# Float16 pairs in the first FFN product, and units of two f tiles: a fused local attention and FFN on one core

## The chip, the cores and the metric

The kernel runs on one core of one Trainium2 chip. The metric is the device time of one execution in microseconds (us); lower is better. Engines are named as the profile names them: PE is TensorE's matmuls and PEld its weight loads, DVE is VectorE, ACT is ScalarE, POOL is GpSimd, SP is the engine whose queue issues the DMAs. A line such as L700 is line 700 of the kernel before.

## The reference

Four batches, eight heads, 768 positions, head size 64. Each query sees the keys at a distance under 16 and, beside them, 24 block keys (the maximum over 32 keys each, with log 32 added to the score) whose values are block means. The 3072 x 512 attention output goes through an FFN of width 2048.

```python
scores_l = scale * np.matmul(q, k.transpose(0, 1, 3, 2))       # masked to |i - j| < 16
scores_s = scale * np.einsum('bhsd,bhnd->bhsn', q, k_sum) + np.log(block)
a = softmax(concatenate([scores_l, scores_s]))                 # spelled out in the original
attn = np.matmul(a, concatenate([v, v_sum]))
x = attn.transpose(0, 2, 1, 3).reshape(3072, 512)
h = x @ w_in                                                   # 512 x 2048
g = h * (1.0 / (1.0 + np.exp(-h)))
out = (g @ w_out).astype(np.float32)                           # 2048 x 512
```

The inputs reach the device as float64, seen there as int64; the kernel takes the weights apart by bits.

## The kernel before

**Precision.** Each factor of an FFN product is kept as a high and a low part, and three products are added up: high by high, high by low, low by high. Both parts are float32r (a float32 that TensorE reads in one pass) in both FFN products. The scores of batches 1 to 3 and their products with v use float16 pairs in the same manner.

**FFN tiling.** Tokens come in 12 chunks of 256 (`CH`); the width 2048 in 16 tiles f of 128 (`NFT`). One step of the FFN, `job_f(i, c, f)`, is one chunk and one f:

- `ffn1` (L700): 4 blocks of the 512 inputs by 3 products, 12 matmuls of 256 columns, each with its own 128x128 weight load, into one half of a PSUM bank `h`;
- ACT takes tanh(h/2) into `t` (L709), DVE makes t = (t + 1)h (L710), which is twice silu, ACT rounds it to `gh` (L711), POOL or DVE takes the rest `gl` = t - gh (L216, a helper of all subtractions);
- `ffn2` (L705): for each of the two 128-token halves 3 matmuls of 512 columns, added up over all f in a PSUM bank;
- after the last f, the bank is copied out times 0.5 (L730 on ACT, L731 on DVE) and stored.

The order is: chunks 0 and 1 over the first 8 tiles f (`QF`), chunks 1 and 0 over the other 8, then one chunk after the other over all 16. So there are 192 steps. `ffn1` of step i waits for `ffn2` of step i - 3 (`APART`); rings of 3 buffers hold `t` (`NT2`) and 4 hold `gh` and `gl` (`NG`). Two chunks of x (`xh`, `xl`) are held at a time.

**Weights.** `job_w(f, kind)` loads the 512 columns of one f tile of one weight matrix (kind 0 is w_in, kind 1 is w_out) by one DMA of 512 KB, rebuilds a float32 from the two words of each float64 in a staging half (ACT L664 and L659, DVE L666), copies it to the high part (ACT L209, DVE L213) and subtracts for the low part (DVE L216). Four staging halves, in two of the three `raw` buffers, are in turn. It is done once, in the first part of the execution; until a weight tile is loaded, its space serves as staging for early attention data.

**Attention** goes by 24 stages of 128 tokens (two for each chunk): scores (L545 in float32 for batch 0, L547 and L548 in float16 pairs after it) of two heads at a time, score + mask and row minimum (DVE L552), exponential and sum (ACT L555), scaling (L566 ACT, L568 POOL, L570 DVE), rest (DVE L594), a DMA transposition, the product with v (L626), and x split into `xh` (ACT L644) and `xl` (DVE L645). Batches 1 to 3 are scaled by powers of two found on the chip (`job_scale`, `v_scale`, whose small matmul is L396), and x is brought back to its own scale at L644 and L645.

**What sets the order.** Nothing is ordered by hand. `Plan` collects all operations with a cost in ns, the engines that may run them, their dependencies and a priority, simulates them several times, and issues them in the order of the best sweep, which also picks the engine where there is a choice. Each engine then runs its own instructions strictly in that order. The priorities hold some twenty offsets (`TUNE`). In the first microseconds idle PE time is filled with matmuls of no use (L286), and spare PSUM bank 6 (`sbank`) takes the scores and the small matmuls; bank 3 joins it when chunk 0 has finished.

Of the kernel before, what the change touches and what calls it, by code (L numbers as in the profile page):

```python
# [34 lines left out]
NFT = DFF // P  # L35
NCT = DM // P
# [9 lines left out]
QF = 8  # L46
AHEAD = 0
NPL = 2
APART = 3
# [153 lines left out]
def local_attn_ffn(ctx: ExitStack, tc: tile.TileContext, qkT, qF, qD, kF, kD, v, vR, w, out):  # L203
# [10 lines left out]

    def less(e, out, in0, in1):
        eng[e].tensor_tensor(out=out, in0=in0, in1=in1, op=ALU.subtract)  # L216
# [10 lines left out]
    wr = [wp.tile([P, DM, 2], U32, name="wt") for _ in range(2 * NFT)] if wide else None  # L227
# [3 lines left out]
    nc.vector.memset(ones, 1.0)  # L231

# [22 lines left out]
    NRAW, NP, NTT, NE, NG, NT2 = 3, 4, 8, 3, 4, 3  # L255
# [21 lines left out]
    xh_t = ring(NSUP, [P, NCT, CH], F32R, "xh")  # L277
    xl_t = ring(NSUP, [P, NCT, CH], F32R, "xl")
    part_t = [const.tile([P, 2, DM], F32, name=f"part{i}") for i in range(NSUP - 2)]
    t_t = ring(NT2, [P, CH], F32, "t")  # L280
    gh_t = ring(NG, [P, CH], F32R, "gh")
    gl_t = ring(NG, [P, CH], F32R, "gl")
# [99 lines left out]
    def v_scale(b, prio):  # L382
# [9 lines left out]
            lambda e: nc.vector.tensor_scalar(out=sc2[:, 3:4], in0=sc2[:, 1:2], scalar1=1.0 / PSC, scalar2=None, op0=ALU.mult))  # L392
# [4 lines left out]
        plan.op({"dve": 67}, lambda e, k=k: nc.vector.tensor_copy(out=vsc_t[b % 2], in_=bank[k][:, :2]), r=[("bank", k)], w=[("vsc", b % 2)], prio=prio)  # L397

# [116 lines left out]
    def tt_of(m):  # L515
        if m < 16 and wide:
            f, kind = tt_late[m // 2 % 4]
            buf, key = wr[2 * f + kind].rearrange("p c i -> p (c i)").bitcast(F32)[:, m % 2 * 4 * P:(m % 2 + 1) * 4 * P], ("w", f, kind, m % 2)
        else:
            return tt_t[m % NTT].rearrange("p (a b) -> p a b", a=6), ("tt", m % NTT)  # L520
        if m < 4 * NPL:
            return buf.rearrange("p (a b) -> p a b", a=4), key
        return buf.bitcast(F16)[:, :6 * P].rearrange("p (a b) -> p a b", a=6), key

    def job_a(m, prio):
# [70 lines left out]
        plan.op({"dve": 672}, low, r=er + sums, w=[("p", pk), ("p", pk, "half")], prio=prio)  # L596
        plan.op({"dma": 672}, lambda e: nc.sync.dma_start_transpose(out=tt, in_=pt.rearrange("p a b -> p (a b)")), r=[("p", pk), ("p", pk, "half")], w=[ttk], prio=prio)

    def job_c(m, prio):
# [28 lines left out]
        plan.op({"pe": 1560}, mm, r=[ttk for _, ttk in parts] + [("v1", s % 2), ("v2", s % 2)], w=[("bank", 7)], prio=prio, cols=2560)  # L628

    def job_x(s, prio):  # L630
# [13 lines left out]
        plan.op({"act": 500}, lambda e: nc.scalar.activation(out=xh, in_=x3, func=AF.Copy, scale=by), r=[("bank", k), vk], w=[("xh", z, half)], prio=prio)  # L644
        plan.op({"dve": 602}, lambda e: nc.vector.scalar_tensor_tensor(out=xl, in0=x3, scalar=by, in1=xh.bitcast(F32), op0=ALU.mult, op1=ALU.subtract),  # L645
                r=[("bank", k), ("xh", z, half), vk], w=[("xl", z, half)], prio=prio, port=())

    def job_w(f, kind, prio):
        prio += nudge("w", f, kind)
        (wf, key), src = half_staging(), w[f][:, kind * DM:(kind + 1) * DM]  # L650
        if wide:
            rt = wr[2 * f + kind]
            low, top = rt[:, :, 0], rt[:, :, 1]
            wu = wf.bitcast(U32)
            plan.op({"dma": 1650}, lambda e: nc.sync.dma_start(out=rt.rearrange("p c i -> p (c i)"), in_=src.bitcast(U32)), w=[("w", f, kind)] + [("w", f, kind) + x for x in ((0,), (1,), (0, "side"), (1, "side"))], prio=prio - TUNE["w_dma"] + nudge("wd", f, kind))
# [6 lines left out]


            plan.op({"act": 575}, lambda e: nc.scalar.activation(out=wf, in_=top.bitcast(F32), func=AF.Prelu, scale=REBIAS, alpha=-SIGN), r=[("w", f, kind)], w=key, prio=prio)  # L664
            plan.op({"act": 575, "dve": 335}, last_bits, r=[("w", f, kind)], w=[("wb", f, kind)], prio=prio)
            plan.op({"dve": 602}, lambda e: nc.vector.scalar_tensor_tensor(out=wu, in0=wu, scalar=3, in1=low, op0=ALU.logical_shift_left, op1=ALU.bitwise_or), r=[("w", f, kind), ("wb", f, kind)], w=key, prio=prio)  # L666
# [7 lines left out]
        plan.op({"act": 527, "dve": 335}, hi, r=key, w=[("w", f, kind), "walloc"], prio=prio)
        prio += nudge("wl", f, kind)
        plan.op({"dve": 602}, lambda e: less(e, wt[f, kind][:, 1, :], wf, wt[f, kind][:, 0, :].bitcast(F32)),
                r=key + [("w", f, kind)], w=[("wl", f, kind)], prio=prio)

    first = list(range(NFT))[:QF]
    rest = list(range(NFT))[QF:]  # L680
# [4 lines left out]
    need_c = {c: order.index((c, 0)) for c in range(NCHUNK)}  # L685
    need_f = {f: min(i for i, cf in enumerate(order) if cf[1] == f) for f in range(NFT)}

    def job_f(i, c, f):
        late = i + TUNE["ffn2"] + nudge("f2", i)
        k, j, n, z = nxt("h", 2) if c < NSUP else nxt("late h", 3), i % NT2, i % NG, slot[c]  # L690
        h, t, gh, gl = bank[k][:, :CH], t_t[j], gh_t[n], gl_t[n]
# [3 lines left out]
        opens, closes = f == 0 or (split and f == QF), f == NFT - 1 or (split and f == QF - 1)  # L695

        def ffn1(e):
            for ct in range(NCT):
                for q, (part, x) in enumerate(((0, xh), (0, xl), (1, xh))):
                    nc.tensor.matmul(out=h, lhsT=wt[f, 0][:, part, ct * P:(ct + 1) * P], rhs=x[:, ct, :], start=(ct == 0 and q == 0), stop=(ct == NCT - 1 and q == 2))  # L700

        def ffn2(u):
            def go(e):
                for q, (g, part) in enumerate(((gh, 0), (gh, 1), (gl, 0))):
                    nc.tensor.matmul(out=bank[ob[u]], lhsT=g[:, u * P:u * P + P], rhs=wt[f, 1][:, part, :], start=(opens and q == 0), stop=(closes and q == 2))  # L705
# [3 lines left out]
        plan.op({"act": 264}, lambda e: nc.scalar.activation(out=t, in_=h, func=AF.Tanh, scale=0.5), r=[("bank", k)], w=[("t", j)], prio=i - TUNE["post"])  # L709
        plan.op({"dve": 335}, lambda e: nc.vector.scalar_tensor_tensor(out=t, in0=t, scalar=1.0, in1=h, op0=ALU.add, op1=ALU.mult), r=[("bank", k)], w=[("t", j)], prio=i - TUNE["post"], port=())  # L710
        plan.op({"act": 307}, lambda e: nc.scalar.copy(out=gh, in_=t), r=[("t", j)], w=[("gh", n)], prio=i - TUNE["post"])  # L711
# [156 lines left out]
```

## Time and profile before

| | |
|---|---|
| time, median of 3 runs | 690.64 us (688.04, 690.64, 694.74) |
| profiled execution | span 694.0 us, from the first to the last instruction; no time of its own beside the span is given for it |
| busy time | PE 667.1, PEld 574.5, DVE 478.4, ACT 432.2, POOL 203.0 us |
| granted TensorE clock, mean | 0.982 |
| read from and written to HBM | 70.34 MB and 6.29 MB |

The span of the profiled execution lies 3.4 us above the median and within the three runs. Busy time of PE is the union of matmuls that overlap in a pipeline, so that PE may be marked busy where it isn't at its peak: the distance from the start of one matmul to the start of the next says more. In the views, a group's row ends with its busy time and the mean length of one instruction, and after a second bar the idle time of the engine before it and who ended that.

### The profile page before, as it was taken

The page shows a single profiled execution, that of the slowest core. Times are in us where ns is not written, and L with a number is a line of the kernel's source. Part 1 is how long each engine was busy: PE and PEld are TensorE (multiplying, and loading weights), DVE is VectorE, ACT ScalarE, POOL GpSimd, SP SyncE. Part 2 cuts the span into 40 slices and gives each one's busy share as a digit, 9 for nine tenths or more (in the row PEclk, how much of TensorE's full clock was granted, in tenths as well). Part 3 has the DMA queues.
Part 4 walks back from the last instruction along what each step waited for, and adds up shares of the span by engine and source line. Part 5 has one row for each costly group of instructions (what it writes and reads, how often), then busy time and mean ns, then how long its engine had stood idle before and what let it go on. Part 6 is the DMA issues. An engine that isn't in the chain of part 4 may idle for free. (4 is left out here: it accounts for less than half of the span.)

```text
span 694.0 us, 14248 instructions
## 1 busy us (share of the span) xinstructions
PE 667.1 (96%) x4941; PEld 574.5 (83%) x4941; DVE 478.4 (69%) x1493; ACT 432.2 (62%) x1141; POOL 203.0 (29%) x267
## 2 busy tenths in 40 slices
PE   8998899999989999999999999999999999999997
PEld 3667779888878798878888888888889888999996
DVE  4688978688799657978894556978895883423332
ACT  4779999686667746756675536767864753422322
POOL 2142156335634042425351111415341230000000
PEclk9679999999999999999999999999999999999999
DMA  7869893967667843774675423665573250100000
GB/s 259 292 152 253 306 323 103 219 180 183 159 147 116 244 119 100 199 136 118 142 192 151 125 85 115 178 141 155 139 171 106 52 114 30 43 1 1 32 1 30
DMA packets 101354, 97.41 MB, mean 140 GB/s; under 512 B 76950, under 2 KB 80022, under 8 KB 101282
## 3 DMA queue, kind: packets, MB, share of 16 engines
q1 hardware_dynamic: 101282, 96.51, 52.5%
q8 instruction: 38, 0.62, 0.4%
q14 instruction: 34, 0.28, 0.1%
HBM read 70.34 MB, written 6.29 MB: 110 GB/s over the span
## 5 line engine op out<-in xcount | busy, mean ns | idle before, releaser
L700 PE MATMUL bank<-xh,wt 128*128 128x256 f32 x1536 | 309.5, 285 | 4.1 <-DVE t L710 2.8
L700 PEld LDWEIGHTS bank<-xh,wt 128*128 128x128 f32 x1536 | 251.6, 191 | 13.9 <-DVE t L710 4.3
L705 PE MATMUL bank<-wt,gh 128*128 128x512 f32 x768 | 247.6, 404 | 2.1 <-ACT gh L711 2.1
L700 PE MATMUL bank<-xl,wt 128*128 128x256 f32 x768 | 217.1, 283 | 0.0
L216 POOL TENSOR_TENSOR gl<-t,gh 128x256 fp32r<-128x256 f32 x115 | 98.1, 855 | 269.0 <-ACT gh L711 218.2
L705 PE MATMUL bank<-wt,gl 128*128 128x512 f32 x384 | 151.1, 393 | 1.6 <-DVE gl L216 1.2
L700 PEld LDWEIGHTS bank<-xl,wt 128*128 128x128 f32 x768 | 146.6, 191 | 6.2
L705 PEld LDWEIGHTS bank<-wt,gh 128*128 128x128 f32 x768 | 131.0, 190 | 20.7 <-ACT gh L711 3.0
L710 DVE SCALAR_TENSOR_TENSOR t<-t,bank 128x256 f32<-128x256 f32 x192 | 79.6, 416 | 85.8 <-ACT t L709 84.7
L709 ACT ACTIVATE t<-bank 128x256 f32<-128x256 f32 x192 | 72.3, 377 | 83.3 <-PE bank L700 81.6
L711 ACT CAST gh<-t 128x256 fp32r<-128x256 f32 x192 | 76.9, 402 | 67.2 <-DVE t L710 66.4
L594 DVE SCALAR_TENSOR_TENSOR p<-e,sum,p 128x128 f16<-128x128 f32 x352 | 109.7, 373 | 4.1 <-ACT p L566 2.6
L555 ACT ACTIVATE e<-e,mx 128x182 f32<-128x182 f32 x192 | 84.1, 439 | 31.2 <-DVE mx L552 29.3
L705 PEld LDWEIGHTS bank<-wt,gl 128*128 128x128 f32 x384 | 72.4, 189 | 20.7 <-POOL gl L216 2.5
L216 DVE TENSOR_TENSOR gl<-t,gh 128x256 fp32r<-128x256 f32 x77 | 37.5, 488 | 33.9 <-ACT gh L711 16.9
L568 POOL TENSOR_SCALAR p<-e,sum 128x182 f16<-128x182 f32 x77 | 35.5, 468 | 75.9 <-DVE sum L561 44.8
L552 DVE CUSTOM_DVE_ANT_0 e<-bank,masks,qsc 128x182 f32<-128x182 f32 x144 | 53.2, 399 | 6.5 <-PE bank L548 6.1
L216 POOL TENSOR_TENSOR vv<-raw,vv 128x1024 f16<-128x1024 f32 x16 | 35.2, 2202 | 13.0 <-ACT t L709 6.7
L566 ACT ACTIVATE p<-e,sum 128x182 f16<-128x182 f32 x81 | 33.6, 440 | 7.5 <-issue 3.6
L555 ACT ACTIVATION_READ_ACCUMULATOR e<-e,mx 128x1 f32 x192 | 36.2, 189 | 0.0
L451 DVE SCALAR_TENSOR_TENSOR qk<-raw,qsc,qk 64x1264 f16<-64x1264 f32 x18 | 28.6, 1588 | 8.8 <-ACT qk L450 8.4
L547 PE MATMUL bank<-qk 128*128 128x182 f16 x144 | 28.4, 245 | 4.8 <-DVE mx L552 2.5
(123 smaller groups left out, 685.3 us busy)
## 6 DMA issues: line engine op xcount, KB each, us to landing
wt<-in_w_dram SPq DMA_DIRECT2D x32, 512.0 KB
raw<-in_kD_dram SPq DMA_DIRECT2D x18, 632.0 KB
raw<-in_v_dram SPq DMA_DIRECT2D x20, 512.0 KB
raw<-in_qD_dram SPq DMA_DIRECT2D x18, 512.0 KB
out_dram<-raw SPq DMA_DIRECT2D x24, 256.0 KB
raw<-in_kF_dram SPq DMA_DIRECT2D x12, 384.0 KB
raw<-in_qF_dram SPq DMA_DIRECT2D x9, 512.0 KB
raw<-in_vR_dram SPq DMA_DIRECT2D x12, 384.0 KB
```

Source lines behind the costliest of these rows:

```text
L216: eng[e].tensor_tensor(out=out, in0=in0, in1=in1, op=ALU.subtract)
L451: plan.op({"dve": 1450}, lambda e: nc.vector.scalar_tensor_tensor(out=kst[64:, :, :NLOC], in0=kr[64:], scalar=qs[64:, 1:2], in1=kst[64:, : ...
L552: plan.op({"dve": 258 if b == 0 else 323}, lambda e, i=i: nc.vector.tensor_tensor_reduce(out=et[:, i, :], in0=sc[:, i, :NKEY], in1=mask, s ...
L555: plan.op({"act": 431}, lambda e, i=i, h=h: nc.scalar.activation(out=et[:, i, :], in_=et[:, i, :], func=AF.Exp, scale=-1.0, bias=mx[:, i:i ...
L566: nc.scalar.activation(out=out, in_=et[:, i, :], func=AF.Copy, scale=by)
L568: nc.gpsimd.tensor_scalar(out=out, in0=et[:, i, :], scalar1=by, scalar2=0.0, op0=ALU.mult, op1=ALU.add)
L594: nc.vector.scalar_tensor_tensor(out=pt[:, i, to:to + z - a], in0=et[:, i, a:z], scalar=su[:, i:i + 1], in1=pt[:, i, a:z], op0=ALU.mult, o ...
L700: nc.tensor.matmul(out=h, lhsT=wt[f, 0][:, part, ct * P:(ct + 1) * P], rhs=x[:, ct, :], start=(ct == 0 and q == 0), stop=(ct == NCT - 1 an ...
L705: nc.tensor.matmul(out=bank[ob[u]], lhsT=g[:, u * P:u * P + P], rhs=wt[f, 1][:, part, :], start=(opens and q == 0), stop=(closes and q == 2))
L709: plan.op({"act": 264}, lambda e: nc.scalar.activation(out=t, in_=h, func=AF.Tanh, scale=0.5), r=[("bank", k)], w=[("t", j)], prio=i - TUN ...
L710: plan.op({"dve": 335}, lambda e: nc.vector.scalar_tensor_tensor(out=t, in0=t, scalar=1.0, in1=h, op0=ALU.add, op1=ALU.mult), r=[("bank", ...
L711: plan.op({"act": 307}, lambda e: nc.scalar.copy(out=gh, in_=t), r=[("t", j)], w=[("gh", n)], prio=i - TUNE["post"])
```

## The change

1. x and w_in become float16 pairs. x is scaled by a power of two for each batch: `xh` and `xl` take `vsc_t` (batch 0, first two stages) or the constant 1/PSC, and stay scaled. w_in is scaled by a power of two for each pair of f tiles, found on the chip: an absolute maximum on DVE, two small matmuls that add it up over the partitions, one bit operation. tanh undoes both scales (`asc_t`, one value per unit and batch); what is left of x's scale goes into the copy of the output. `ffn2` keeps float32r; w_out is scaled by the inverse power.
2. Two neighbouring f tiles form one unit: `ffn1` fills the two halves of one PSUM bank (two groups of 12 matmuls), and tanh, t, gh and gl handle 512 columns at once; `ffn2` adds 6 matmuls for each token half. `QF`, `APART`, `NT2` and `NG` become 4, 2, 2 and 3 units.
3. Weights are loaded and converted by pairs, 1024 columns at a time, with DMAs of 1 MB; two whole staging buffers are in turn.
4. Some costs given to `Plan` and all the offsets in `TUNE` have other values.

The core of the diff:

```diff
+NFP = NFT // 2
-QF = 8
+QF = 4
-APART = 3
+APART = 2
+    def times(e, out, in_, by):       # ACT Copy with scale, POOL or DVE tensor_scalar
+    def rest_of(out, in_, by, less):
+        nc.vector.scalar_tensor_tensor(out=out, in0=in_, scalar=by, in1=less, op0=ALU.mult, op1=ALU.subtract)
-    NRAW, NP, NTT, NE, NG, NT2 = 3, 4, 8, 3, 4, 3
+    NRAW, NP, NTT, NE, NG, NT2 = 3, 4, 8, 3, 3, 2
-    xh_t = ring(NSUP, [P, NCT, CH], F32R, "xh")
+    xh_t = ring(NSUP, [P, NCT, CH], F16, "xh")
-    t_t = ring(NT2, [P, CH], F32, "t")
+    t_t = ring(NT2, [P, 2 * CH], F32, "t")
-    def half_staging():
-        i = nxt("half", 2 * (NRAW - 1))
+    def low_staging():
+        i = nxt("low", NRAW - 1)
+        return raw[i][:, :2 * DM], [("raw", i, 0), ("raw", i, 1)]
...
+        by, need = (vsc_t[b % 2][:, 0:1], [("vsc", b % 2)]) if s < NPL else (1.0 / PSC, [])
+        plan.op({"act": 575}, lambda e: times(e, xh, x3, by), ...)
+        plan.op({"dve": 661}, lambda e: rest_of(xl, x3, by, xh), ...)
...
+            plan.op({"dma": 3300}, lambda e: nc.sync.dma_start(out=rt.rearrange("p c i -> p (c i)"), in_=src.bitcast(U32)), ...)
+        u, r = ur_t[:, fp, 0:1], ur_t[:, fp, 1:2]
+        if kind == 0:
+            plan.op({"dve": 1160}, lambda e: nc.vector.tensor_reduce(out=wm_t[:, fp:fp + 1], in_=wf, axis=AX.X, op=ALU.max, apply_absolute_value=True), ...)
+            k = sbank()
+            def gather(e):
+                nc.tensor.matmul(out=bank[k][:, :2], lhsT=spread, rhs=wm_t[:, fp:fp + 1].to_broadcast([P, 2]), start=True, stop=False)
+                nc.tensor.matmul(out=bank[k][:, :2], lhsT=spread, rhs=least.to_broadcast([P, 2]), start=False, stop=True)
+            plan.op({"pe": 240}, gather, ...)
+            plan.op({"dve": 170}, ... out=ur_t[:, fp, :] ... bitwise_and 0x7F800000, bitwise_xor flip ...)
+            plan.op({"pool": 250, "dve": 130}, lambda e: times(e, asc_t[0][:, fp:fp + 1], u, vsc_t[0][:, 1:2]), ...)
+        by = u if kind else r
         def hi(e):
-            copy(e, wt[f, kind][:, 0, :], wf)
+            times(e, flat(0), wf, by)
-                less(e, wt[f, kind][:, 1, :], wf, wt[f, kind][:, 0, :].bitcast(F32))
+                rest_of(flat(1), wf, by, flat(0))
...
+        def ffn1(d):
+            def go(e):
+                for ct in range(NCT):
+                    for q, (part, x) in enumerate(((0, xh), (0, xl), (1, xh))):
+                        nc.tensor.matmul(out=h[:, d * CH:(d + 1) * CH], lhsT=wt[f, 0][:, part, d, ct * P:(ct + 1) * P], rhs=x[:, ct, :], ...)
...
-        plan.op({"act": 264}, lambda e: nc.scalar.activation(out=t, in_=h, func=AF.Tanh, scale=0.5), ...)
+        plan.op({"act": 590}, lambda e: nc.scalar.activation(out=t, in_=h, func=AF.Tanh, scale=asc_t[c // 3 % 2][:, f:f + 1]), ...)
-        plan.op({"pool": 742, "dve": 340}, lambda e: less(e, gl, t, gh.bitcast(F32)), ...)
+        plan.op({"pool": 1280, "dve": 605}, lambda e: less(e, gl, t, gh.bitcast(F32)), ...)
```

More of the change, by code (lines that the diff above doesn't have):

```diff
@@ L213, in copy @@
             eng[e].tensor_copy(out=out, in_=in_)
+    def times(e, out, in_, by):
+        if e == "act":
+            nc.scalar.activation(out=out, in_=in_, func=AF.Copy, scale=by)
+        elif e == "pool":
+            nc.gpsimd.tensor_scalar(out=out, in0=in_, scalar1=by, scalar2=0.0, op0=ALU.mult, op1=ALU.add)
+        else:
+            nc.vector.tensor_scalar(out=out, in0=in_, scalar1=by, scalar2=None, op0=ALU.mult)
+    def rest_of(out, in_, by, less):
+        nc.vector.scalar_tensor_tensor(out=out, in0=in_, scalar=by, in1=less, op0=ALU.mult, op1=ALU.subtract)
     def less(e, out, in0, in1):
@@ L226, in local_attn_ffn, with raw_w @@
     wt = {}
-    wr = [wp.tile([P, DM, 2], U32, name="wt") for _ in range(2 * NFT)] if wide else None
+    wr = [wp.tile([P, 2, DM, 2], U32, name="wt") for _ in range(2 * NFP)] if wide else None
+    def raw_w(f, kind):
+        return wr[2 * (f // 2) + kind][:, f % 2].rearrange("p c i -> p (c i)")
     ident = const.tile([P, P], F32, name="ident")
@@ L231, in local_attn_ffn @@
     nc.vector.memset(ones, 1.0)
+    spread = const.tile([P, P], F32, name="spread")
+    nc.vector.memset(spread, 2.0 ** -13)
+    least = const.tile([P, 1], F32, name="least")
+    nc.vector.memset(least, 2.0 ** -80)
+    flip = const.tile([P, 2], U32, name="flip")
+    nc.vector.memset(flip[:, 0:1], 0)
+    nc.vector.memset(flip[:, 1:2], 0x7F800000)
+    wm_t = const.tile([P, NFP], F32, name="wm")
+    ur_t = const.tile([P, NFP, 2], F32, name="ur")
+    asc_t = [const.tile([P, NFP], F32, name=f"asc{i}") for i in range(2)]
     blocks = const.tile([P, 11 * 4], F32, name="blocks")
@@ L397, in v_scale @@
         plan.op({"dve": 67}, lambda e, k=k: nc.vector.tensor_copy(out=vsc_t[b % 2], in_=bank[k][:, :2]), r=[("bank", k)], w=[("vsc", b % 2)], prio=prio)
+        if b:
+            plan.op({"pool": 250, "dve": 150}, lambda e: times(e, asc_t[b % 2], ur_t[:, :, 0], vsc_t[b % 2][:, 1:2]),
+                    r=[("vsc", b % 2)] + [("ur", f) for f in range(NFP)], w=[("asc", b % 2, f) for f in range(NFP)], prio=prio)
     def job_v(b, prio):
@@ L670, in hi @@
-        def hi(e):
-            wt[f, kind] = wp.tile([P, 2, DM], F32R, name="wt")
-            copy(e, wt[f, kind][:, 0, :], wf)
[L674 to L680, printed above, removed]
+            plan.op({"act": 1000}, lambda e: nc.scalar.activation(out=wf, in_=top.bitcast(F32), func=AF.Prelu, scale=REBIAS, alpha=-SIGN), r=mine, w=key, prio=prio)
@@ L681, in local_attn_ffn @@
+        plan.op({"act": 1040, "dve": 700}, hi, r=key + [("ur", fp)], w=mine + ["walloc"], prio=prio)
+        prio += nudge("wl", fp, kind)
+        plan.op({"dve": 1190}, lambda e: rest_of(flat(1), wf, by, flat(0).bitcast(F32) if kind else flat(0)),
+                r=key + mine + [("ur", fp)], w=[("wl", fp, kind)], prio=prio)
+    first = list(range(NFP))[:QF]
+    rest = list(range(NFP))[QF:]
     runs = [(c, first) for c in range(NSUP)] + [(c, rest) for c in reversed(range(NSUP))]
@@ L684, in local_attn_ffn @@
     slot = [c if c < NSUP else NSUP - 1 - c % NSUP for c in range(NCHUNK)]
-    need_c = {c: order.index((c, 0)) for c in range(NCHUNK)}
-    need_f = {f: min(i for i, cf in enumerate(order) if cf[1] == f) for f in range(NFT)}
+    need_c = {c: 2 * order.index((c, 0)) for c in range(NCHUNK)}
+    need_f = {f: 2 * min(i for i, cf in enumerate(order) if cf[1] == f) for f in range(NFP)}
     def job_f(i, c, f):
-        late = i + TUNE["ffn2"] + nudge("f2", i)
+        at = 2 * i
+        late = at + TUNE["ffn2"] + nudge("f2", i)
         k, j, n, z = nxt("h", 2) if c < NSUP else nxt("late h", 3), i % NT2, i % NG, slot[c]
-        h, t, gh, gl = bank[k][:, :CH], t_t[j], gh_t[n], gl_t[n]
+        h, t, gh, gl = bank[k], t_t[j], gh_t[n], gl_t[n]
         xh, xl = xh_t[z], xl_t[z]
@@ L694, in job_f @@
         split = c < NSUP - 2
[L695 to L700, printed above, removed]
+        opens, closes = f == 0 or (split and f == QF), f == NFP - 1 or (split and f == QF - 1)
@@ L702, in ffn2 @@
+        have = [("w", 2 * f + d, kind) for d in range(2) for kind in range(2)]
+        def ffn1(d):
+            def go(e):
+                for ct in range(NCT):
+                    for q, (part, x) in enumerate(((0, xh), (0, xl), (1, xh))):
+                        nc.tensor.matmul(out=h[:, d * CH:(d + 1) * CH], lhsT=wt[f, 0][:, part, d, ct * P:(ct + 1) * P], rhs=x[:, ct, :], start=(ct == 0 and q == 0), stop=(ct == NCT - 1 and q == 2))
+            return go
         def ffn2(u):
             def go(e):
-                for q, (g, part) in enumerate(((gh, 0), (gh, 1), (gl, 0))):
-                    nc.tensor.matmul(out=bank[ob[u]], lhsT=g[:, u * P:u * P + P], rhs=wt[f, 1][:, part, :], start=(opens and q == 0), stop=(closes and q == 2))
@@ L711, in job_f @@
-        plan.op({"act": 307}, lambda e: nc.scalar.copy(out=gh, in_=t), r=[("t", j)], w=[("gh", n)], prio=i - TUNE["post"])
-        plan.op({"pool": 742, "dve": 340}, lambda e: less(e, gl, t, gh.bitcast(F32)), r=[("t", j), ("gh", n)], w=[("gl", n)], prio=i - TUNE["post"])
+                for d in range(2):
+                    for q, (g, part) in enumerate(((gh, 0), (gh, 1), (gl, 0))):
+                        nc.tensor.matmul(out=bank[ob[u]], lhsT=g[:, d * CH + u * P:d * CH + u * P + P], rhs=wt[f, 1][:, part, d, :], start=(opens and d == 0 and q == 0), stop=(closes and d == 1 and q == 2))
@@ new lines, in ffn2 @@
+            return go
+        for d in range(2):
+            plan.op({"pe": 1310}, ffn1(d), r=[(x, z, half) for x in ("xh", "xl") for half in range(2)] + have[2 * d:2 * d + 1] + [("wl", f, 0)] + ([("turn", i - APART)] if i >= APART else []), w=[("bank", k)], prio=at + nudge("f1", i), cols=3072)
+        plan.op({"act": 590}, lambda e: nc.scalar.activation(out=t, in_=h, func=AF.Tanh, scale=asc_t[c // 3 % 2][:, f:f + 1]), r=[("bank", k), ("asc", c // 3 % 2, f)], w=[("t", j)], prio=at - TUNE["post"])
@@ L713, in job_f @@
+        plan.op({"dve": 605}, lambda e: nc.vector.scalar_tensor_tensor(out=t, in0=t, scalar=1.0, in1=h, op0=ALU.add, op1=ALU.mult), r=[("bank", k)], w=[("t", j)], prio=at - TUNE["post"], port=())
+        plan.op({"act": 515}, lambda e: nc.scalar.copy(out=gh, in_=t), r=[("t", j)], w=[("gh", n)], prio=at - TUNE["post"])
+        plan.op({"pool": 1280, "dve": 605}, lambda e: less(e, gl, t, gh.bitcast(F32)), r=[("t", j), ("gh", n)], w=[("gl", n)], prio=at - TUNE["post"])
         for u in range(2):
-            plan.op({"pe": 690}, ffn2(u), r=[("gh", n), ("gl", n), ("w", f, 1), ("wl", f, 1)], w=[("bank", ob[u])] + ([("turn", i)] if u else []), prio=late, cols=1536)
@@ L715, in job_f @@
-        if closes and f == NFT - 1:
+            plan.op({"pe": 1380}, ffn2(u), r=[("gh", n), ("gl", n), have[1], have[3], ("wl", f, 1)], w=[("bank", ob[u])] + ([("turn", i)] if u else []), prio=late, cols=3072)
+        if closes and f == NFP - 1:
             stg, key = staging()
@@ L778, in local_attn_ffn @@
         job_out(s, False)
-    for f in range(NFT):
+    for f in range(NFP):
         for kind in range(2):
@@ L788, in local_attn_ffn @@
         job_f(i, c, f)
-        if c == 0 and f == NFT - 1:
+        if c == 0 and f == NFP - 1:
             spare[0] = 1
-        if d and f == NFT - 1:
+        if d and f == NFP - 1:
             job_out(2 * d, True)
@@ L795, in local_attn_ffn @@
     plan.issue()
-TUNE = dict(km=51.75, w_dma=-83.25, w_dec=-134.75, a0=-32.0, a1=-18.5, d1=1.75, span=6.75, post=31.75, ffn2=37.5, jc0=-43.75, jc1=-28.25, jx0=-127.0, jx1=2.75, vs=68.0, qk=27.75, k=-29.0, v=160.25, v0=43.0, out=37.75, first=14.5)
+TUNE = dict(km=63.6, w_dma=-32.67, w_dec=-94.38, a0=-34.94, a1=-3.24, d1=26.9, span=-13.29, post=30.75, ffn2=36.75, jc0=-22.12, jc1=-86.81, jx0=-123.15, jx1=-88.6, vs=82.84, qk=20.41, k=-20.15, v=153.19, v0=36.41, out=33.18, first=17.74)
 NUDGE = {}
```

84 lines of the change are left out of this document (42 added, 42 removed).

## The prediction

> **What bounds the kernel now.** I read the busy times of the page first, then the windows, then the chain of work that ended last.
>
> ```profile
> PE 667.1 (96%) x4941; PEld 574.5 (83%) x4941; DVE 478.4 (69%) x1493; ACT 432.2 (62%) x1141; POOL 203.0 (29%) x267
> ...
> 0.00:50.00 50.00, 45.39 (x233) 27.38 (x234) 32.73 (x147) 32.82 (x100) 15.03 (x35) 0.81 0.75 238
> 50.00:100.00 50.00, 44.36 (x320) 36.43 (x318) 43.08 (x110) 46.80 (x104) 16.07 (x19) 0.95 0.95 290
> 100.00:150.00 50.00, 49.87 (x343) 43.76 (x341) 38.49 (x92) 40.96 (x102) 22.27 (x26) 1.00 0.65 171
> ...
> 200.00:250.00 50.00, 46.98 (x399) 41.05 (x398) 38.30 (x115) 34.07 (x91) 14.81 (x19) 1.00 0.67 158
> ...
> 600.00:650.00 50.00, 50.00 (x351) 45.30 (x350) 15.69 (x35) 15.36 (x38) 1.48 (x2) 1.00 0.06 20
> ```
>
> PE is marked busy for 667.1 of 694.0 us. In each window row the columns are PE, PEld, DVE, ACT and POOL, then the granted clock and the DMA engines' share. PE is idle 10.3 us in the first 100 us, where ACT (46.8 of 50) and the DMA engines (0.95) are full with the weights; later it is nearly always busy at clock 1.00. A busy pipeline can still be slow, so I looked at the distances in the chain:
>
> ```profile
> 584.29 1.43 PE bank L700 x12
> 585.72 1.39 PE bank L705 x6
> 587.11 1.43 PE bank L700 x12
> ...
> 685.53 4.80 PE bank L705 x21
> 690.35 0.60 ACT raw L730
> ```
>
> The pieces stand end to end: one FFN step is 1.43 + 1.39 = 2.82 us of PE and nothing between. From 582.6 us to the end the chain is this alone. 192 steps are 541 us of the span, so the FFN's matmul stream is the bound, and a matmul of L700 takes 1430 / 12 = 119.2 ns.
>
> **The float16 product.** `ffn1` keeps its 2304 matmuls, 256 columns and separate weight loads; only the type changes. The trace has float16 matmuls with a full 128x128 weight load each, of 182 columns:
>
> ```profile
> 194.31 0.24 PE L548 MATMUL bank<-qk 128*128 128x182 f16 x1
> ...
> 194.78 0.24 PE L548 MATMUL bank<-qk 128*128 128x182 f16 x1
> ...
> 512.06 1.24 PE bank L626 x40
> ```
>
> Between these two starts lie six distances (L548 and L547 in turn): 0.47 / 6 = 78.3 ns. By columns, 256 cost 78.3 x 256 / 182 = 110.1 ns. That is 9.1 ns less than now, and 2304 x 9.1 = 21.0 us. From the other row: L626 puts 40 matmuls of 128 columns on halves of the array, 20 pairs in 1.24 us, 62 ns a pair; by columns 256 would cost 124 ns, 4.8 more than now (11 us lost). A line through the two float16 rows (78.3 at 182, 62 at 128) gives 100.6 at 256 (43 us won). I take 110.1: the same full array and the same weight load, and L626 has a weight load for every 31 ns, which makes it the less alike. The Trainium skill, "TensorE: Matmul & The Clock Gate", section "Back-to-back issue gap", says that a sustained stream of weight loads and matmuls spaces out to about 81 ns at 128 columns and 131 at 512; between them 256 would be at 98 ns and the gain 49 us. Here L705, 512 columns with a load each, stands at 1390 / 6 = 231.7 ns, so this trace doesn't agree, and I keep that rule as a rival of small chance only.
>
> **The scale of w_in** adds 16 matmuls of two columns on PE. Nearest is the small matmul of `v_scale`:
>
> ```profile
> L396 PE MATMUL bank<-sc,ones 1*128 1x2 f32 x8 | 1.5, 256 | 0.0
> L328 DVE TENSOR_REDUCE km<-raw 128x24 f32<-128x768 f32 x12 | 11.4, 951 | 6.2 <-DMA raw<-in_kF_dram 6.1
> L445 ACT ACTIVATE qk<-raw,qsc 128x1024 f16<-128x1024 f32 x18 | 20.6, 1143 | 7.4 <-DMA raw<-in_qD_dram 6.8 <-PE bank L547 0.6
> L446 DVE SCALAR_TENSOR_TENSOR qk<-raw,qsc,qk 128x1024 f16<-128x1024 f32 x18 | 23.2, 1291 | 6.7 <-ACT qk L445 6.7
> L664 ACT ACTIVATE raw<-wt 128x512 f32<-128x512 f32 x32 | 21.4, 679 | 0.8 <-DVE wt L216 0.8
> L666 DVE SCALAR_TENSOR_TENSOR raw<-raw,wt 128x512 uint32<-128x512 uint32 x32 | 25.2, 795 | 0.2 <-ACT raw L664 0.2
> L216 DVE TENSOR_TENSOR wt<-raw,wt 128x512 fp32r<-128x512 f32 x32 | 23.6, 745 | 0.1
> ```
>
> 8 took 1.5 us, so 16 take 3; they may all lie in PE's idle time (10.3 us in the first 100) or, if every one stalls PE for its 256 ns, cost 4.1. I take 1.5. On DVE, eight maxima over 1024 columns at 951 x 1024 / 768 = 1268 ns are 10.1 us. The pair conversion itself: L666 and L216 were 32 x (795 + 745) = 49.3 us and become 32 operations like L446, 32 x 1291 = 41.3 us. With some 2 us of small operations DVE has about 4 us more in the weight part, ACT less: its 679 ns for 512 columns grow, at the 0.85 ns a column of the next fence, to some 1115, so two passes on 16 pairs save about 16 x 2 x 243 = 7.8 us; the high part (L209, 621 x 2 against L445's 1143) another 1.6. ACT is the fuller of the two there, so I count the sum as nothing, with 5 us either way. The x operations keep their size, and the 1 MB DMAs move the same bytes on the same SP queue with half the issues.
>
> **Post-processing by 512 columns** moves ACT and DVE, not PE:
>
> ```profile
> L709 ACT ACTIVATE t<-bank 128x256 f32<-128x256 f32 x192 | 72.3, 377 | 83.3 <-PE bank L700 81.6 <-POOL gl L216 0.8
> L710 DVE SCALAR_TENSOR_TENSOR t<-t,bank 128x256 f32<-128x256 f32 x192 | 79.6, 416 | 85.8 <-ACT t L709 84.7
> L711 ACT CAST gh<-t 128x256 fp32r<-128x256 f32 x192 | 76.9, 402 | 67.2 <-DVE t L710 66.4 <-DVE sc L392 0.7
> L209 ACT CAST wt<-raw 128x512 fp32r<-128x512 f32 x30 | 18.6, 621 | 0.0
> L645 DVE SCALAR_TENSOR_TENSOR xl<-bank,vsc,xh 128x512 fp32r<-128x512 f32 x22 | 16.4, 745 | 2.2 <-ACT xh L644 2.2
> ```
>
> The cast of 512 columns takes 621 against 402 for 256 (0.85 ns a column). So a unit's gh takes 621 for 804 before, its tanh 377 + 219 = 596, with about 100 more for a scale read per partition, for 754; ACT saves 0.24 us a unit, 23 us over 96 units. DVE's t takes 745 (L645, also from PSUM) for 832, 8 us in all. ACT goes to about 400 us and DVE stays near 475. Neither ends the time as long as PE is full, so I cost this at nothing; the cover is PE's own stream. The new wait is `ffn2`'s: it needs both tiles of a unit through a longer chain (in the tail below, 1.74 us becomes about 2.7), and what is queued behind it on PE is everything, the next unit's `ffn1` and the scores. The order gives it one unit of cover, 2.64 us of `ffn1` and 2.78 of `ffn2`, twice what is needed, except at the end:
>
> ```profile
> 685.25 0.28 PE L700 MATMUL bank<-xh,wt 128*128 128x256 f32 x1
> 685.63 0.39 ACT L709 ACTIVATE t<-bank 128x256 f32<-128x256 f32 x1 [0.85 <-PE bank L700]
> 686.94 0.43 DVE L216 TENSOR_TENSOR gl<-t,gh 128x256 fp32r<-128x256 f32 x1 [0.47 <-ACT gh L711]
> ```
>
> Now tanh starts at 685.63 and gl ends at 687.37, under five half steps of L705 (3.4 us). After, about 3.0 us from the last `ffn1` matmul stand over the 2.78 us of one unit's `ffn2`: 0.2 us shows, 0.8 if POOL takes that gl. I add 0.3.
>
> **Sum**, against the profiled span: -21.0 + 1.5 + 0.3 = -19.2. A part of PE's remaining waits (27 us idle, 2.8 of L700's 4.1 us on DVE's t) should shrink with 23 us less on ACT; I count 2 of them, so -21.2: 694.0 becomes 672.8. The span stands 3.4 us above the median, so on the median's footing 690.6 - 21.2 = 669.4; I say **669**.
>
> **Rivals.** (1) *The attention feed holds the end.* The chain of waits isn't PE's everywhere:
>
> ```profile
> PE 28%; DVE 6%; DMA 4%; ACT 2%; issue 1%; SPq 0%; POOL 0%; ACTq 0%; DVEq 0%
> ...
> 566.22 3.16 DVE p L594 x4
> ...
> 570.85 4.44 DMA raw<-in_v_dram
> ```
>
> It can be followed back to 402 us; PE has 28% of the span in it, 194 of those 292 us. If faster matmuls help only there, two thirds of 21.0 remain: -14.0 + 1.8 = -12.2, 678. For it: at 542 to 582 us the chain runs over DVE, ACT and a DMA. Against it: PE is busy 49.3 of 50 us in that very window, and DVE's work is no more than before.
>
> (2) *Slower: the two staging buffers.* A w_in pair holds one from the rebuild to its low part: by the rows 1.1 + 1.3 + 1.3 (maximum) + about 1 for the small matmul and its hand-overs + 1.1 + 1.3, with hand-overs some 8 us; a w_out pair some 5.3. Through two buffers that is 6.7 us a pair if nobody waits. Before, conversion ran from 21 to 119 us, 12.2 us for two tiles. The eighth pair then comes at 21 + 8 x 12.2 = 119 us again, about when it is wanted. If the engines' queues stretch a pair beyond 12.2 us, each us costs 8 at PE; from 14.8 us on the gain is gone, and at 15.8 the time is 669 + 29 = 698. For it: DVE 43 and ACT 47 of 50 us are busy there, and the small matmul waits in PE's queue and for bank 6, which the scores use. Against: 6.7 is little more than half of 12.2.
>
> (3) *It doesn't do what it says*: a matmul stays at 119 ns because the moving data sets it. Then -2 + 1.8, 690; with the 124 ns of L626 it is 701. (4) *More*: 100.6 ns a matmul or the waits gone, 645 to 658; the rule on spacing taken whole gives 641.
>
> **Chances.** The forecast (659 to 677) 0.62, rival 1 (677 to 684) 0.16, rival 2 0.06, rival 3 0.08, rival 4 0.08, of which the rule on spacing has 0.01. About 1% is what a measurement of this kernel can tell from no change (6.9 us; the three runs lie 1% apart): faster, under 683.7, 0.84 (forecast, rival 4 and all of rival 1 but 0.02); within, 0.09 (those 0.02, 0.06 of rival 3, 0.01 of rival 2); slower, over 697.5, 0.07 (the rest of rivals 2 and 3). The range 655 to 686 leaves out about 0.05 below and 0.13 above.
>
> **What would show it.** Right: L700's twelve matmuls at 1.32 us in the chain, L705's unchanged at 231.7 ns each; ACT's busy time near 400 us, DVE's near 475, PE still over 94% busy; the last `ffn2` pieces still end to end. Rival 1: idle rows of PE after 150 us that end with `tt`, `xl` or L626's operands. Rival 2: PE idle beyond 15 us before 130, ended by `wt` or `ur`. Wrong altogether: L700 at 1.43 again.

## The result and the profile after

The changed kernel takes 667.64 us (median of 4 runs, 665.2 to 668.73), the kernel before 692.69 in the runs beside it (688.04 to 696.19): a ratio of 0.966, 95% interval 0.961 to 0.970, so some 25 us less. The forecast was 669 in a range of 655 to 686. The profiled execution took 666.79 us, with a span of 665.0. Beside the experiments below, the kernel before ran from 684.94 us at a mean granted clock of 0.999 to 697.46 us at 0.978; its profiled execution had 0.982 and that of the changed kernel 0.990, and the two spans lie 29.0 us apart, more than the medians.

First the page of the changed kernel (busy times, then the shares of the chain that ended last):

```profile
PE 644.5 (97%) x5023; PEld 516.3 (78%) x5023; DVE 465.2 (70%) x1342; ACT 408.1 (61%) x894; POOL 219.4 (33%) x232
...
PE 65%; DVE 4%; DMA 3%; issue 1%; POOL 1%; ACT 1%; SPq 0%; POOLq 0%; ACTq 0%
```

PE is still the full engine, and its share of the chain went from 28% to 65%: the chain can now be followed back to 162 us (402 before), and most of it is PE's. Its last pieces (start, length, line, count; L748 is `ffn1`, 24 matmuls a unit, L755 `ffn2`, 12):

```profile
642.32 2.63 PE bank L748 x24
644.95 2.77 PE bank L755 x12
...
654.38 6.85 PE bank L755 x30
```

In most pieces of the chain `ffn1` takes 2.64 us for two f tiles (2.63 in the one shown), 1.32 for one, 110.0 ns a matmul; `ffn2` stands at 2.77 / 12 = 231 ns as before. The stages in windows (PE, PEld, DVE, ACT, POOL busy; clock; DMA share), first of after, then the long one of before:

```profile
0.00:50.00 50.00, 46.29 (x275) 28.81 (x275) 35.85 (x174) 34.39 (x105) 12.26 (x39) 0.93 0.84 257
50.00:100.00 50.00, 41.64 (x352) 33.51 (x348) 44.42 (x52) 42.11 (x49) 28.01 (x18) 0.93 0.89 300
100.00:150.00 50.00, 49.42 (x315) 39.65 (x314) 34.67 (x79) 32.02 (x59) 19.50 (x19) 1.00 0.45 122
...
150.00:665.00 515.00, 507.11 (x4090) 414.30 (x4088) 350.28 (x1039) 299.60 (x684) 159.60 (x157) 1.00 0.49 123
```

```profile
150.00:694.00 544.00, 527.46 (x4051) 466.93 (x4049) 364.06 (x1149) 311.60 (x839) 149.66 (x190) 1.00 0.46 115
```

After 150 us PE is idle 515.0 - 507.1 = 7.9 us, against 16.5 before (each with 3.7 to 3.8 us behind the last matmul). In the first 150 us it is idle 12.7 us, against 10.4. So the 29.0 us between the two spans are 21 of shorter matmuls (192 x 0.11), 8.6 of fewer late waits, 2.3 lost early; 1.7 are left over. The clock granted in the first 50 us (0.93 for 0.81) lies on that side; the new small matmuls (L699 and L700 below, 6.2 us of busy time) and 50 more of the filling matmuls lie on the other, and nothing here splits them. Who ended the early waits is in the groups by line (busy, mean ns; idle time before, by whom):

```profile
L699 PE MATMUL bank<-wm,spread 128*128 128x2 f32 x16 | 3.1, 261 | 7.9 <-DVE wm L695 7.9
L700 PE MATMUL bank<-least,spread 128*128 128x2 f32 x16 | 3.1, 264 | 0.0
L760 ACT ACTIVATE t<-bank,asc 128x512 f32<-128x512 f32 x96 | 65.5, 682 | 88.7 <-PE bank L748 88.5
L761 DVE SCALAR_TENSOR_TENSOR t<-t,bank 128x512 f32<-128x512 f32 x96 | 65.6, 684 | 69.8 <-ACT t L760 69.3
L762 ACT CAST gh<-t 128x512 fp32r<-128x512 f32 x96 | 59.0, 614 | 39.0 <-DVE t L761 36.9 <-PE bank L577 1.0 <-DVE xl L225 0.8
```

L699 (a line of the changed kernel, as all in this view) is the small matmul that spreads the maximum of w_in: PE stood 7.9 us in front of it.

### The profile page after: what moved, and what is told of

It reads as the page before. It is cut to its first block, busy times and chain, and to the rows that moved or that the text cites. A ratio compares the mean times of both kernels' runs of the same rounds, so it can differ in the third digit from the quotient of the medians.

```text
span 665.0 us, 13761 instructions
## 1 busy us (share of the span) xinstructions
PE 644.5 (97%) x5023; PEld 516.3 (78%) x5023; DVE 465.2 (70%) x1342; ACT 408.1 (61%) x894; POOL 219.4 (33%) x232
## 4 chain that ended last, share of the span: by engine, by line
PE 65%; DVE 4%; DMA 3%; issue 1%; POOL 1%; ACT 1%; SPq 0%; POOLq 0%; ACTq 0%
PE bank L755 30%; PE bank L748 29%; PE bank L655 3%; PE bank L576 1%; PE bank L577 1%; DVE p L623 1%; DMA raw<-in_qD_dram 1%; DMA raw<-in_v_dram 1%; DVE e L581 1%; POOL gl L228 1%; DMA raw<-in_kF_dram 0%; DMA tt<-p 0%; DMA out_dram<-raw 0%; DVE qk L475 0%; DVE qk L480 0%
## 5 line engine op out<-in xcount | busy, mean ns | idle before, releaser
L748 PE MATMUL bank<-xh,wt 128*128 128x256 f16 x1536 | 269.9, 273 | 0.0
L748 PEld LDWEIGHTS <-wt 128*128 128x128 f16 x2304 | 218.5, 98 | 44.4 <-issue 19.5
L755 PE MATMUL bank<-wt,gh 128*128 128x512 f32 x768 | 251.1, 408 | 0.3 <-ACT gh L762 0.3
L748 PE MATMUL bank<-xl,wt 128*128 128x256 f16 x768 | 209.3, 273 | 0.8 <-DVE xl L225 0.8
L755 PEld LDWEIGHTS bank<-wt,gh 128*128 128x128 f32 x768 | 136.3, 190 | 25.9 <-issue 0.6
L755 PE MATMUL bank<-wt,gl 128*128 128x512 f32 x384 | 152.3, 397 | 2.1 <-POOL gl L228 2.0
L228 POOL TENSOR_TENSOR gl<-t,gh 128x512 fp32r<-128x512 f32 x60 | 88.1, 1468 | 116.0 <-ACT gh L762 113.8
L760 ACT ACTIVATE t<-bank,asc 128x512 f32<-128x512 f32 x96 | 65.5, 682 | 88.7 <-PE bank L748 88.5
L761 DVE SCALAR_TENSOR_TENSOR t<-t,bank 128x512 f32<-128x512 f32 x96 | 65.6, 684 | 69.8 <-ACT t L760 69.3
L755 PEld LDWEIGHTS bank<-wt,gl 128*128 128x128 f32 x384 | 72.6, 189 | 21.0 <-POOL gl L228 4.4
L762 ACT CAST gh<-t 128x512 fp32r<-128x512 f32 x96 | 59.0, 614 | 39.0 <-DVE t L761 36.9
L228 DVE TENSOR_TENSOR gl<-t,gh 128x512 fp32r<-128x512 f32 x36 | 30.3, 840 | 23.4 <-ACT gh L762 23.4
L589 DVE TENSOR_SCALAR sum<-sum 128x2 f32<-128x2 f32 x96 | 26.1, 282 | 10.0 <-ACT e L584 9.4
L655 PEld LDWEIGHTS <-vv 128*64 128x64 f16 x880 | 25.3, 110 | 5.4 <-issue 4.5
```

Source lines behind the costliest of these rows:

```text
L655: nc.tensor.matmul(out=av[j * D:(j + 1) * D, i * P:(i + 1) * P], lhsT=vt[:, vi, h * D:(h + 1) * D], rhs=tt[:, j * 3 + blk, :], start=(n == ...
L748: nc.tensor.matmul(out=h[:, d * CH:(d + 1) * CH], lhsT=wt[f, 0][:, part, d, ct * P:(ct + 1) * P], rhs=x[:, ct, :], start=(ct == 0 and q == ...
L755: nc.tensor.matmul(out=bank[ob[u]], lhsT=g[:, d * CH + u * P:d * CH + u * P + P], rhs=wt[f, 1][:, part, d, :], start=(opens and d == 0 and ...
L760: plan.op({"act": 590}, lambda e: nc.scalar.activation(out=t, in_=h, func=AF.Tanh, scale=asc_t[c // 3 % 2][:, f:f + 1]), r=[("bank", k), ( ...
L761: plan.op({"dve": 605}, lambda e: nc.vector.scalar_tensor_tensor(out=t, in0=t, scalar=1.0, in1=h, op0=ALU.add, op1=ALU.mult), r=[("bank", ...
L762: plan.op({"act": 515}, lambda e: nc.scalar.copy(out=gh, in_=t), r=[("t", j)], w=[("gh", n)], prio=at - TUNE["post"])
```

## The experiments

Twelve kernels, each timed beside the kernel before, whose median lay between 688.8 and 691.6 in the three sets; the ratios compare best. "Late idle" is PE's idle time after 150 us, from a window as above; it includes the time behind the last matmul (3.7 to 3.8 us in the two kernels), which the "late waits" of the expectations leave out.

| run | first product | unit | offsets | costs told to the plan | median us | ratio (95%) | late idle us |
|---|---|---|---|---|---|---|---|
| before | float32r | one f | old | old | 690 | 1 | 16.5 |
| the change | float16 | two f | new | new | 667.6 | 0.966 (0.961 to 0.970) | 7.9 |
| 1 | float32r | two f | new | new | 685.5 | 0.990 (0.984 to 0.996) | 6.3 |
| 2, halves of 256 | float16 | two f | new | new | 666.7 | 0.963 (0.958 to 0.968) | 9.4 |
| 3, no wait for max | float16 | two f | new | new | 663.6 | 0.959 (0.954 to 0.964) | 7.7 |
| 4 | float16 | one f | old | old | 681.3 | 0.985 (0.980 to 0.990) | 26.1 |
| 5 | float16 | two f | old | new | 675.5 | 0.981 (0.977 to 0.984) | 15.7 |
| 6 | float16 | one f | new | three new | 662.1 | 0.961 (0.958 to 0.965) | 10.5 |
| 7 | float16 | one f | old | three new | 664.5 | 0.963 (0.959 to 0.968) | 12.2 |
| 8, max held back | float16 | two f | new | new | 680.2 | 0.987 (0.984 to 0.991) | 13.1 |
| 9 | float32r | one f | old | two new | 685.7 | 0.994 (0.991 to 0.998) | 15.4 |
| 10 | float16 | one f | old | first product's | 676.1 | 0.981 (0.976 to 0.985) | 20.2 |
| 11 | float16 | one f | old | two new | 681.5 | 0.987 (0.981 to 0.993) | 25.5 |
| 12 | float16, both products | one f | new | four new | 653.5 | 0.948 (0.944 to 0.953) | 19.3 |

**1. The type undone.**

```diff
-    xh_t = ring(NSUP, [P, NCT, CH], F16, "xh")
+    xh_t = ring(NSUP, [P, NCT, CH], F32R, "xh")
...
-                wt[fp, kind] = home.bitcast(F16)...
+                wt[fp, kind] = wp.tile([P, 2, 2, DM], F32R, name="wt")
```

> The changed kernel with float32r again in the first FFN product (x and w_in), all else kept: pair units, 512-column post-processing, the scales, and the same order of instructions on every engine. To fit the memory x's low part is made but not read; the high part stands in its place in the second of the three products. Theory A (the type sets the distance of the matmuls, and PE's stream sets the end): the 12 matmuls of one f take 1.43 us again for 1.32, 192 x 0.11 = 21 us, so 667.6 + 21 = 689 (685 to 693). Rival B (units and the new order gave the gain, the type little): 667 to 675.

685.5 us. The chain of this run shows a unit's `ffn1` at 2.87 us, 119.6 ns a matmul:

```profile
666.25 2.87 PE bank L748 x24
669.13 1.39 PE bank L755 x6
```

Its late window:

```profile
150.00:684.00 534.00, 527.68 (x4097) 468.79 (x4095) 348.77 (x1040) 301.65 (x684) 158.93 (x158) 1.00 0.47 119
```

The span grew from 665.0 to 684.0, 19 us, of the 22 that 96 x 0.23 makes; PE's idle time fell by 2.4, 1.6 of it late. Theory A holds for this order, B is out.

**2. The post-processing in halves of 256 columns.**

```diff
-  nc.scalar.activation(out=t, in_=h, func=AF.Tanh, scale=...)
+  [nc.scalar.activation(out=t[:, s], in_=h[:, s], func=AF.Tanh, scale=...) for s in two]
```

The t, gh and gl steps are split in the same way.

> The changed kernel with every 512-column step of the post-processing (tanh, t, gh, gl) as two instructions of 256 columns in the same place of the order. ACT gets some 30 us of fixed costs back, DVE and POOL some 15 to 25. Theory C (the wider post-processing is why PE waits less after 150 us, 4 us against 13 before): most of those 9 us return, 672 to 677. Rival D (PE's stream covers it, the waits went for another reason): only the tail grows, 667.6 + 0.5 to 1.5 = 668 to 669.

666.7 us, no slower. The groups of this run show that the fixed costs did come back:

```profile
L761 ACT ACTIVATE t<-bank,asc 128x256 f32<-128x256 f32 x192 | 79.7, 466 | 79.4 <-PE bank L749 78.8 <-PE bank L577 0.6
L763 ACT CAST gh<-t 128x256 fp32r<-128x256 f32 x192 | 69.1, 404 | 26.7 <-DVE t L762 26.3 <-PE bank L577 0.2
```

ACT is busy 20 us longer, DVE 18, POOL 16, the late idle time is 9.4 us for 7.9, and the end doesn't move. Theory C falls: 512 columns at a time aren't why PE waits less.

**3 and 8. The wait for the maximum.** Run 3 reads a constant in L699's place:

```diff
-  rhs=wm_t[:, fp:fp + 1].to_broadcast([P, 2])
+  rhs=level.to_broadcast([P, 2])              # level: a tile filled with 0.2
```

> The changed kernel, but the small matmuls that spread the scale of w_in read a constant instead of the maximum, which is still computed: PE's order is kept and its wait for the maximum (7.9 us of idle time in the first 100 us) can't occur. The scale is then no longer found from the data. Theory E (that wait is on the path): 667.6 - 5 to 8 = 660 to 663. Rival F (PE then waits for the same weights a little later, because DMA, ACT and DVE set the pace of the weights): 666 to 668.

663.6 us, 4 less than the change, between the two expectations, and the intervals of the two ratios overlap, so the 4 us are not clear of noise. PE's idle time in its first 150 us fell by 2.6 us only, because other waits took over (PE's waits of `ffn2` for gh and gl rose from 2.4 to 5.8 us). The rest of the 6.3 us between the two profiled spans is PE's busy time (641.0 for 644.5), with a granted clock of 0.97 for 0.93 in the first 100 us; whether the wait and the clock hang together isn't shown.

```profile
L757 PE MATMUL bank<-wt,gh 128*128 128x512 f32 x768 | 250.8, 408 | 1.2 <-ACT gh L764 1.2
L757 PE MATMUL bank<-wt,gl 128*128 128x512 f32 x384 | 152.2, 396 | 4.6 <-POOL gl L228 4.5
```

Run 8 keeps the maximum and has the plan issue the small matmul later, by a step "gap" of 3 us that no engine does:

```diff
+  plan.op({"gap": 3000}, lambda e: None, r=[("wm", fp)], w=[("wm late", fp)], prio=prio, port=())
-  plan.op({"pe": 240}, gather, r=[("wm", fp)], ...)
+  plan.op({"pe": 240}, gather, r=[("wm late", fp)], ...)
```

> The changed kernel, complete, with one line in the plan: the small matmul that spreads the scale of w_in is held to be ready 3 us later than the maximum, so that it is issued further back in PE's order. Theory E (PE's 7.9 us of waits for the maximum are partly on the path; a constant in place of the maximum gave 663.6): those waits fall below 3 us and the time to 661 to 665. Rival F (the weights come later by the same amount and PE waits for them): 666 to 669. Everything later in the order may move by 1 to 2 us either way.

680.2 us. The waits for `wm` did fall, from 7.9 to 1.4 us, but one changed time in the plan drew another order for the whole kernel, and that order is 12 us worse. The expectation had allowed 1 to 2 us for that. Of the 11.5 us between the profiled spans, 6.1 are more idle time of PE, 5.2 of them late, and 5.4 more busy time. What makes this order worse was not found.

**4. Float16 alone in the old kernel.**

```diff
-    xh_t = ring(NSUP, [P, NCT, CH], F32R, "xh")
+    xh_t = ring(NSUP, [P, NCT, CH], F16, "xh")
...
-            wt[f, kind] = wp.tile([P, 2, DM], F32R, name="wt")
+            wt[f, kind] = ... if kind else ....bitcast(F16)...
```

> The kernel before with one part of the change alone: x and w_in as float16 pairs in the first FFN product, single f tiles, old order and old costs, no scales (so the low parts lose some bits). Theory A: the matmul distance falls to 110 ns here too, 692.7 - 21 = 671.6 (668 to 675), and the units and the order are worth the other 4 us. Rival 1 of the prediction (the attention feed holds the end of the old order): two thirds of it, 692.7 - 14 = 679 (676 to 683).

681.3 us: the gain is 10, not 21. The matmuls did get shorter; PE's late window shows where the rest went, and the list of PE's waits after 150 us (for whom, total us, times, longest) that they are mostly for attention (all but L706, which is `ffn2`; L384 belongs to the scale of v):

```profile
150.00:679.60 529.60, 503.52 (x3990) 395.52 (x3988) 357.07 (x1118) 303.96 (x818) 146.39 (x182) 1.00 0.46 114
```

```profile
PE bank L547 <- DVE mx L552: 4.8, 8, 1.6
PE bank L384 <- DVE am L380: 3.7, 2, 2.6
PE bank L547 <- DVE qk L451: 3.5, 3, 1.5
PE bank L706 <- ACT gh L712: 3.4, 4, 1.7
```

That is 26.1 us of late idle time for 16.5, and 4 more early. The scores (L547) stand in PE's order at a place that PE now reaches before DVE has freed the bank or made `qk`.

**5, 6 and 7. Units, offsets or costs.** Run 5 is the changed kernel with the old `TUNE`. Run 6 is run 4 with the new `TUNE` and three costs; run 7 has the three costs alone:

```diff
-  plan.op({"pe": 1430}, ffn1, ...)
+  plan.op({"pe": 1310}, ffn1, ...)
-  plan.op({"dve": 672}, low, ...)
+  plan.op({"dve": 900}, low, ...)
-  plan.op({"pe": 1560}, mm, ...)
+  plan.op({"pe": 1400}, mm, ...)
```

> The changed kernel with the offsets of the kernel before in TUNE; pair units, float16 and costs stay. Float16 alone in the old order gave 681.3, with 22 us of PE waits after 150 us against 4 in the changed kernel. Theory S (the pair units keep PE fed: longer units, deeper buffers, fewer operations to place): 666 to 671, late waits under 8 us. Theory O (the offsets do it): 676 to 685, late waits 13 to 22 us.

> The kernel before with float16 in the first FFN product, single f tiles, no scales, and now the offsets and the three corrected costs of the changed kernel (first product 1310, low part of p 900, product with v 1400). Theory O (the order does it): 667 to 672, late waits under 8 us. Theory S (the units do it): 678 to 685, late waits of 15 to 22 us as with float16 alone.

> As the run before it, but with the old offsets: float16, single f tiles, and only the three costs corrected, so that the plan knows of the shorter first product. If the waits come from a plan that still reckons 1430 ns for 12 matmuls: 668 to 674. If they come from the offsets or from the single units: 679 to 684, as with float16 alone.

675.5, 662.1 and 664.5 us. Run 5 is just under the range of theory O, and runs 6 and 7 are some 4 us below every range. Theory S falls: single f tiles get all of the gain, pairs with old offsets don't. Runs 6 and 7 have neither scales nor pairs of weights, and no run separates these two. The new offsets aren't needed, since run 7 has the old ones; but with pairs the old ones leave 15.7 us of late idle time, though run 5 has the new costs. In run 7 the late idle time is

```profile
150.00:665.50 515.50, 503.31 (x4011) 397.43 (x4009) 357.94 (x1126) 306.58 (x820) 155.82 (x191) 1.00 0.48 119
```

This is 12.2 us, with the same operations as run 4: only their order, who does the work where the plan may choose, and the number of filling matmuls (117 for 77) differ.

**9, 10 and 11. Which cost.**

> The kernel before, float32r and old offsets, with two costs of the plan corrected (low part of p 900 for 672, product with v 1400 for 1560): a control with no change of type. Theory K (the waits of float16 alone came from a plan that doesn't know of the shorter first product): nothing is gained here, 686 to 694. Theory L (these two costs, or any newly drawn order, make the difference): 678 to 684.

> Float16 alone, with one cost of the plan corrected: the first product of one f tile 1310 for 1430 ns. Theory K: 664 to 671, late PE waits under 12 us. Theory L: 677 to 683, as with float16 alone.

> Float16 alone, with the two other costs corrected (low part of p 900, product with v 1400) and the first product still at 1430. Theory K: 676 to 683. Theory L: 664 to 671.

685.7, 676.1 and 681.5 us. The two costs without the first product's bring nothing to float16 (681.5 for 681.3, late idle time 25.5) and 0.6% to float32r. The first product's cost alone brings 5 us by the medians (late idle time 20.2), less than theory K said; by the ratios it is 0.4%, and their intervals overlap. All three bring 17. The late windows of runs 10 and 11:

```profile
150.00:675.20 525.20, 504.99 (x4009) 399.48 (x4006) 366.51 (x1151) 303.57 (x816) 151.72 (x186) 0.99 0.47 118
150.00:678.90 528.90, 503.38 (x3990) 395.88 (x3988) 355.30 (x1124) 309.93 (x823) 149.67 (x179) 1.00 0.48 115
```

So of these four orders only the one with all three costs has few late waits; neither part of the costs alone gives it. Each set of costs was drawn once, and run 8 shows that a new order can move the time by 12 us: how much of the 17 us is due to the true times, and how much to one lucky order, stays open.

**12. Float16 in the second product too** (run 6, and):

```diff
-    gh_t = ring(NG, [P, CH], F32R, "gh")
+    gh_t = ring(NG, [P, CH], F16, "gh")
-        plan.op({"pe": 690}, ffn2(u), ...)
+        plan.op({"pe": 655}, ffn2(u), ...)
```

`gl` and w_out change in the same way.

> Float16 in both FFN products on single f tiles with the new offsets and costs (the run at 662.1), second product's cost 655 for 690; gh, gl and w_out become float16 pairs, no scales, so that low parts lose bits. Theory A (the type sets the distance, and PE's stream the end): by the line through 78.3 ns at 182 columns and 110.0 at 256, 512 columns cost 219.6 for 231.7; 1152 x 12.1 = 14 us, so 648 (644 to 652). Rival (attention's DVE and ACT work now sets the end): 656 to 662, with PE waits after 150 us up from 7 to 15 us or more.

653.5 us, faster than both kernels and than run 6 (0.948, at most 0.953, against at least 0.958). Its chain, and the late windows of run 6 and of this run:

```profile
620.17 1.29 PE bank L706 x6
621.47 1.31 PE bank L701 x12
```

```profile
150.00:659.40 509.40, 498.92 (x3982) 395.12 (x3979) 364.39 (x1121) 307.42 (x829) 154.16 (x189) 1.00 0.47 122
150.00:651.20 501.20, 481.87 (x3988) 333.24 (x3985) 350.37 (x1119) 308.96 (x831) 158.79 (x194) 0.99 0.49 123
```

A matmul of `ffn2` takes 1.29 / 6 = 215.0 ns, less than the 219.6 reckoned: 1152 x 16.7 = 19 us of PE's stream. The span fell by 8.2 (659.4 to 651.2), and late idle time rose from 10.5 to 19.3. As in run 4, about half of what the stream saves comes back as waits, mostly for attention, though here the plan was told the new cost: theory A has the matmuls right, the rival has the waits right, and the time lies between. Without scales, the low parts lose bits where values are small, so runs 4, 6, 7 and 10 to 12 are what the type can give on these inputs, not the whole of the change.

## Why the prediction was right

**The term that carried it** was right: 110.1 ns a matmul from the row of 182-column scores by columns, 110.0 measured; 21.0 us reckoned, 19.0 shown by run 1 in the span and 18 in the medians. The other two bounds (100.6 and 124) weren't met. The rule of the Trainium skill ("TensorE: Matmul & The Clock Gate", section "Back-to-back issue gap") that a sustained stream comes to 131 ns at 512 columns finds no support: with a weight load each, 512 columns take 215.0 ns in float16 (run 12) and 231 in float32r. The same section gives columns over 2.4 GHz plus 2.5 ns for the gap of an isolated matmul, and says that this counts too much at 512 columns; the estimate by it, 109.2 and 215.8 ns, agrees with the float16 rows (110.0 and 215.0), not with the float32r ones.

**"I cost this at nothing; the cover is PE's own stream"** was right for the wider post-processing: run 2 takes 20 us of ACT's relief back and nothing happens. For the same reason the step "A part of PE's remaining waits (27 us idle, 2.8 of L700's 4.1 us on DVE's t) should shrink with 23 us less on ACT; I count 2 of them" had the wrong cause. The late waits shrank by 8.6 us, by the order of the instructions (run 1 has this order with the old type, and 6.3 us), which the prediction gave no term.

**The small matmuls** were mis-sized: 1.5 us reckoned with 4.1 at most, from the length of the instruction. The row was misread, too. A float32 matmul of the program stands twice in these counts: L396 runs once for each of four batches and has x8, and L699 and L700 run once for each of eight pairs and have x16 each. So the 16 new matmuls are 32 in the count and 6.2 us of busy time, not 3. Beside that there was the wait in PE's queue, 7.9 us, for which the sum has no term; taking it away gained about 4, not clear of noise. The tail cost nothing where 0.3 was reckoned: 30 matmuls of `ffn2` in a row end the run.

**The sum** was less exact than it looks. On the spans, where its terms were read, it said 672.8 and 665.0 came, 7.8 us less, mostly because the late waits shrank by 8.6 and not by 2. On the medians it said 21.2 us less, and some 25 came. That 669 lies within 1.4 us of 667.64 is partly luck: in the runs beside the change, the kernel before took 692.69, 2.1 us more than the 690.64 from which the forecast counted down.

**Rival 1**, the attention feed, had 0.16 and 678. It is what happens in the old order: float16 alone gives 681, though the waits end mostly with the scores' `mx` and `qk` and with `am`, not with the `tt`, `xl` or operands of L626 that the prediction named. The forecast's step "192 steps ... the FFN's matmul stream is the bound" was thus only half the condition. PE was 96% busy, and in run 4 the shorter work still uncovered 14 us more of idle time; in the order of the change it uncovered 2 (run 1 against the change). Rival 2 (staging buffers) wasn't seen: the eight maxima start between 33.1 and 116.4 us, 11.9 us a pair, where 12.2 was the pace before; PE's idle time in the first 150 us is 12.7 us, 7.9 of it for the maximum, and no matmul of `ffn1` or `ffn2` waits for weights in the groups. Rival 3 is out by the 110.0.

**Other marks:** ACT at 408 (about 400 reckoned), DVE at 465 (near 475), PE 97%, the last pieces end to end. The tanh of 512 columns takes 682 for 696 reckoned; run 2 shows 466 for 377 at 256 columns, 89 ns for a scale read per partition. The Trainium skill ("ScalarE: Activation LUTs", section "What ACT_TABLE_LOAD costs") has about 93 ns for each such operand, and this trace agrees.

## What to carry to other kernels

Read the distance between starts in a row of the same type and the same weight load, not the busy time: here it gave the price of a changed type to within 1 ns. Where engines run a fixed order made from reckoned times, don't count on the whole of what the full engine saves: in runs 4 and 12 about half came back as its own waits for the side work. Change the reckoned times together with the instruction (run 7 kept all of it), and then look at the waits of the new order, since run 12 lost half although its plan knew the new time. A tiny operation on the full engine can wait longer than it takes, so price the wait as well; and a change that widens side work off that engine can be worth nothing, as here.

## What the runs showed of the hardware

A float32r matmul costs more than a float16 one, and the difference grows with the columns: 119.6 against 110.0 ns at 256 (run 1 and the change), 231 against 215 at 512 (the change and run 12), that is 9.6 and 16 ns more. The weight load takes longer too (191 ns in float32r, 98 in float16, mean of the profiles before and after), but a fixed cost from it would be the same at both widths. Two widths say no more than that, and what causes the difference isn't shown.
